# Sparse attention with routed experts on one core: the mask added by TensorE in PSUM, the row shift by VectorE, and the work resequenced

## The chip, the core and the metric

One NeuronCore of a Trainium2 chip. Its engines run in parallel, each through its own instructions in program order: TensorE (PE) multiplies matrices into PSUM, VectorE (DVE) and ScalarE (ACT) work on SBUF and PSUM, GpSimd (POOL) on SBUF, and SyncE (SP) issues most DMAs. The metric is the device time of one execution in microseconds (us).

## The reference

Attention over 8 batches of 8 heads, 576 positions, 64 features. Heads 0 to 3 see the last 32 positions (a local mask), heads 4 to 7 see every 32nd earlier position (a strided mask). Per batch a gate score picks 128 of the 576 rows, which pass a two-layer network and are added back, weighted by a sigmoid.

```python
scores = scale * np.matmul(q, k.transpose(0, 1, 3, 2))
mask_local = (rel >= 0) & (rel < stride)
mask_strided = (rel >= 0) & (pos[None, :] % stride == pos[:, None] % stride)
scores = np.where(masks[None, :, :, :], scores, -1000000000.0)
scores = scores - np.max(scores, axis=-1, keepdims=True)
attn = np.exp(scores)
attn = attn / (np.sum(attn, axis=-1, keepdims=True) + 1e-09)
out = np.matmul(attn, v)
...
for b in range(B):
    top_idx = np.argpartition(-scores[b], capacity)[:capacity]
    xe = x[b, top_idx]
    ye = np.maximum(xe @ w1, 0.0) @ w2
    g = 1.0 / (1.0 + np.exp(-scores[b, top_idx]))
    out[b, top_idx] = x[b, top_idx] + g[:, None] * ye
```

## The kernel before

The 8 batches are taken as 4 groups of two. A group has four pairs of heads (two strided, S, then two local, L), and each pair is cut into two units, so there are 32 units. A unit holds both heads of a pair (h = 0, 1) for 6 or 5 chunks of 128 query rows (S) or 5 or 4 (L). Only the key columns that a mask lets through are computed: 54 columns a chunk for S, 64 for L.

A unit goes through these steps, which have letters in a string `ORDER`:

- `s`, scores: TensorE multiplies small blocks (64 rows of the array, 32 or 64 columns) into two PSUM banks of pool `ps_s`, one for each head (line L241). VectorE adds the mask from PSUM into SBUF tile `sb` (L254) and takes the maximum of each row and chunk, `mx` (L250); GpSimd subtracts it in `sb` (L251).
- `e`: ScalarE takes the exponential (L266; unit 0 does it in two halves, L257).
- `t`: TensorE transposes 4 to 6 blocks through the one bank of `ps_t` (L284), four and then the rest, each copied out by ScalarE to `at` (L285).
- `v`: TensorE multiplies with the values (L313), ScalarE copies out to `xr` (L318, L320).
- `n`: VectorE takes the reciprocals of the sums (L331, L332), GpSimd scales (L334).
- `g`: for the second pair of a kind VectorE forms the gate scores chunk by chunk, instruction `gt` (L348), and SP stores the attention output.

The step `c` advances the ranking of a group: scores brought into order, `rl` transposes (L432), comparisons `b` on VectorE (L470), counting matmuls `bl` on TensorE (L455), one-hot rows (L490), a matmul that picks row numbers, and two gathers by GpSimd's indirect DMA. After it an expert of that group can run: transposes `xt` (L547), 8 hidden chunks `ph` of 12 matmuls (L565), output `po` in 4 parts of 12 matmuls (L581), and a scatter (L588). The letters `f` and `F` advance experts, `w` the split of the weights into two parts (ScalarE L192, GpSimd L194, L198), `q`, `l` and `r` issue the loads of queries and keys, of values and of weights on SP's queue.

`ORDER` sets the program order of all engines at once: each letter emits the next piece of its kind, and where a piece needs another that has not been emitted, that one is emitted first. Buffers limit how far kinds may run ahead of each other: `NSB = 3` score tiles, 2 tiles `at`, `XR = 2`, `QKS = 2` query and key tiles, `RINGS = 4` value tiles.

Of the kernel before, what the change touches and what calls it, by code (L numbers as in the profile page):

```python
# [9 lines left out]
F32 = mybir.dt.float32  # L10
# [37 lines left out]
def attention_then_expert(ctx: ExitStack, tc, capacity, qkL, qkS, vL, vS, w1, w2, consts, consts16, outL, outS):  # L48
# [5 lines left out]
    ps_s = ctx.enter_context(tc.tile_pool(name="ps_s", bufs=2, space=PSUM))  # L54
    ps_t = ctx.enter_context(tc.tile_pool(name="ps_t", bufs=1, space=PSUM))
    ps_a = ctx.enter_context(tc.tile_pool(name="ps_a", bufs=2, space=PSUM))
    ps_c = ctx.enter_context(tc.tile_pool(name="ps_c", bufs=1, space=PSUM))
    ps_f = ctx.enter_context(tc.tile_pool(name="ps_f", bufs=2, space=PSUM))
# [3 lines left out]
    fill = []  # L62
    done = dict.fromkeys("setvngqlrPC", 0)
# [10 lines left out]
    def keep_warm(k):  # L74
        warm = ps_f.tile([P, 512], F32, tag="f", name="warm")
        for _ in range(k):
            ins = pe.matmul(warm, idle, idle[:, None, :].broadcast_to([P, 4, P]), start=True, stop=True)  # L77
# [4 lines left out]
    loaded = {}  # L82

# [48 lines left out]
    maskS = const(QT, "maskS")  # L132
# [6 lines left out]
    done["q"], done["l"] = 2, 3  # L139
# [3 lines left out]
    sizes = 5 * WL, 9 * NCL + 9, NCL * NCS, P * len(rounds), PERMS  # L143
    cuts = [0, *(sum(sizes[: k + 1]) for k in range(5))]
    small = cp.tile([P, cuts[-1]], BF16, name="small")
    nc.sync.dma_start(small, consts16)
    maskL, tab, column, slot, perms = (small[:, x0:x1] for x0, x1 in zip(cuts, cuts[1:]))
    maskL = maskL.rearrange("p (c w) -> p c w", w=WL)
# [19 lines left out]
    split = [0]  # L168

# [3 lines left out]

    def load_weights(i):
        src = halves[i // 2 if i < 4 else i // 4 + 1][0]
        if i < 4:
            n, at = 1024, i % 2 * 1024
            raws[i] = wk.tile([P, n], F32, tag="hl" if i % 2 else "hh", bufs=1, name=f"raw{i}")
        else:
            n, at = 512, i % 4 * 512  # L180
            raws[i] = xes[:, 2 + i % 2]
        nc.sync.dma_start(raws[i], src[:, at : at + n])

    def split_weights():
        for i in range(12):
            complete("r", i)
            _, hi, lo = halves[i // 2 if i < 4 else i // 4 + 1]
            late = None
            for k in range(0, 1024 if i < 4 else 512, 512):
                at = (i % 2 * 1024 if i < 4 else i % 4 * 512) + k  # L190
                cols, raw = slice(at, at + 512), raws[i][:, k : k + 512]
                act.copy(hi[:, cols], raw)  # L192
                if late:
                    pool.tensor_tensor(*late, ALU.subtract)  # L194
                    split[0] += 1
                late = lo[:, cols], raw, hi[:, cols].bitcast(F32)
                yield
            pool.tensor_tensor(*late, ALU.subtract)  # L198
            split[0] += 1
            yield  # L200
# [7 lines left out]
    gated = [0]  # L208
# [3 lines left out]
    def scores(i):  # L212
# [16 lines left out]
        ps = [ps_s.tile([P, 512], F32, tag="s", name=f"s{i}_{h}") for h in range(2)]  # L229
        M = 32 if kind == "L" else 64  # L230
        for c in range(n):
            for x in range(P // M):
# [6 lines left out]
                for h in range(2):  # L239
                    rows = slice(64 * h, 64 * h + 64)  # L240
                    pe.matmul(  # L241
                        ps[h][M * x : M * x + M, c * W : (c + 1) * W],
                        qk[rows, S2 + q0 : S2 + q0 + M],
                        qk[rows, k0 : k0 + W],
                        start=True,
                        stop=True,
                    )

        def shift(part, peak):
            dve.tensor_reduce(peak, part, axis=AX.X, op=ALU.max)  # L250
            pool.tensor_tensor(part, part, peak[..., None].broadcast_to([*peak.shape, W]), ALU.subtract)  # L251

        for h in range(2):
            dve.tensor_tensor(sv[:, h], ps[h][:, : n * W].rearrange("p (c w) -> p c w", w=W), mk, ALU.add)  # L254
            if i == 0:
                shift(sv[:, h], top[:, h])
                act.activation(sv[:, h], sv[:, h], AF.Exp, scale=0.125)  # L257
            yield
        if i:
            shift(sv, top)  # L260
        yield

    def exponentials(i):
        if i:
            sv = live[i][1]
            act.activation(sv, sv, AF.Exp, scale=0.125)  # L266
        yield

    def transposes(i):
# [4 lines left out]
        at = wk.tile([P, 6, P], F32, tag="at", name=f"at{i}")  # L274
# [5 lines left out]
        for k in range(0, len(blocks), 4):  # L280
            part = blocks[k : k + 4]
            pt = ps_t.tile([P, 4, P], F32, tag="t", name=f"t{i}_{k}")
# [3 lines left out]
            yield  # L286

    def values(i):
# [12 lines left out]
        pa = [ps_a.tile([P, 512], F32, tag="a", name=f"a{i}_{k}") for k in range(2)]  # L301
# [14 lines left out]
        for k in range(2):  # L316
# [7 lines left out]
            yield  # L324

    def normalize(i):
# [8 lines left out]
        yield  # L335

    def gates(i):
        g, kind, hp, c0, c1 = units[i]
        if hp == 0:
            return  # L340
# [5 lines left out]
        for c in range(c0, c1):  # L346
            tmp = wk.tile([P, DM // 2], BF16, tag="tmp", bufs=2, name=f"gt{i}_{c}")
            dve.scalar_tensor_tensor(  # L348
                tmp,
                xf[:, c, :],  # L350
                1.0,
                wg[:, w0 : w0 + DM // 2],
                op0=ALU.mult,
                op1=ALU.mult,
                accum_out=gate[g, kind][:, c : c + 1],
            )
            if (c - c0) % 2 and c + 1 < c1:
                yield
# [7 lines left out]
        gated[0] = i + 1  # L366
        yield

    past = {"hidden": 0, "all": 0}
# [13 lines left out]
    def reorder(g):  # L383
        gs = gate[g, "S"]
# [3 lines left out]
        yield  # L388
# [4 lines left out]
        yield  # L393
        pt = ps_c.tile([P, 4, P], F32, tag="c", name=f"rs{g}")[:, 0, : 3 * NCL]
# [4 lines left out]
        yield  # L399
# [22 lines left out]
    def choose(g):  # L422
        score = wk.tile([P, NCL], F32, tag="score", bufs=1, name=f"score{g}")
        dve.tensor_tensor(score, gate[g, "L"][:, :NCL], natural[g], ALU.add)
        yield
        row = wk.tile([P, S2], F32, tag="row", bufs=1, name=f"row{g}")
        for k in range(0, NCL, 4):
            m = min(4, NCL - k)
            pool_, tag = (ps_c, "c") if not k else (ps_s, "s") if g == NG - 1 else (ps_c, "c") if g else (ps_f, "f")
            pt = pool_.tile([P, 4, P], F32, tag=tag, name=f"rl{g}_{k}")  # L430
# [3 lines left out]
            yield  # L434
# [7 lines left out]
        below = ps_c.tile([P, 4, P], F32, tag="c", name=f"bl{g}")[:, 0, :NCL]  # L442
# [20 lines left out]
        for group in rank_groups:  # L463
# [19 lines left out]
            yield  # L483
        earlier(0)
        yield
        dve.tensor_tensor(rank, rank, below, ALU.add)
        for rd, (r0, m) in enumerate(rounds):
            hot = row.bitcast(BF16)[:, :S2].rearrange("p (c k) -> p c k", k=P)
            for c in range(0, NCL, 3):
# [6 lines left out]
                yield  # L496
            idx = wk.tile([P, 2, 2], I32, tag="idx", bufs=4, name=f"idx{g}_{rd}")
            gt = wk.tile([P, 2], F32, tag="gt", bufs=4, name=f"gate{g}_{rd}")
            pt = ps_c.tile([P, 4, P], F32, tag="c", name=f"ip{g}_{rd}")
            picked = pt.rearrange("p a b -> p (a b)")[:m, :18]  # L500
# [12 lines left out]
            yield  # L513
            if g == 1:
                weights_up_to(16)
            while past["all"] < g - 1:
                take(fill)
            for bb in range(2):
                xe = xes[:, 2 * (g % 2) + bb]
# [8 lines left out]
                if bb and rd == len(rounds) - 1:  # L528
                    fill.append(expert(g))
                    done["C"] += 1  # L530
                yield


    def expert(g):
        last = g == NG - 1
        for rd, (r0, m) in enumerate(rounds):
            n = 2 * m
            while past["hidden"] < g:
                take(fill)
# [295 lines left out]
```

## Time and profile before

| | |
|---|---|
| time, median of 3 runs | 284.45 us (283.52 to 285.22) |
| time of the profiled execution | 281.86 us |
| its span, first to last instruction | 280.1 us |
| busy: TensorE, VectorE, GpSimd, ScalarE | 224.7, 186.0, 155.2, 102.2 us |
| mean granted TensorE clock | 0.858 |
| bytes moved by DMA | 54.18 MB |

The profile is of one execution. Busy time is the time in which an engine has an instruction of the program running. The granted clock is the share of the full TensorE clock in a stretch; it is a mean over two levels, full and half.

### The profile page before, as it was taken

What the parts mean: (1) busy time and instruction counts of PE and PEld (TensorE: products, weight loads), DVE (VectorE), ACT (ScalarE), POOL (GpSimd) and SP (SyncE); (2) the same over time, 40 slices, a digit from 0 to 9 for tenths busy, and PEclk for the clock granted to TensorE, in tenths of its full rate; (3) what the DMA queues carried; (4) which work ended last, traced back from release to release, by engine and by line L of the source; (5) the groups of instructions that cost most, each with busy time, mean ns of one, the idle gap of its engine ahead of it and who ended that gap; (6) DMA issues with size and microseconds to landing.
All of it is one profiled execution on the core that took longest, in us unless ns stands there. A gap on an engine that the chain in (4) does not pass through costs nothing.

```text
span 280.1 us, 10759 instructions
## 1 busy us (share of the span) xinstructions
PE 224.7 (80%) x4714; PEld 186.6 (67%) x4714; DVE 186.0 (66%) x499; ACT 102.2 (36%) x226; POOL 155.2 (55%) x185
## 2 busy tenths in 40 slices
PE   7675776585865885799778798678999999999990
PEld 3554555464754663697676686467889797989980
DVE  0444284776599799977997976947997676432320
ACT  1343461452552355446425254344342130212110
POOL 5327347365584694958946869737268450522014
PEclk9687796768677597599999569979999999999996
DMA  6979665884966099860957978924302410211002
GB/s 207 412 289 343 266 241 153 315 314 163 311 228 264 22 332 386 302 248 11 357 193 291 319 296 250 349 73 133 112 4 77 191 54 0 63 50 39 2 0 75
DMA packets 12566, 54.18 MB, mean 193 GB/s; under 512 B 2104, under 2 KB 2232, under 8 KB 9656
## 3 DMA queue, kind: packets, MB, share of 16 engines
q1 hardware_dynamic: 10984, 49.30, 49.0%
q0 software_dynamic: 1536, 4.20, 4.4%
q8 instruction: 37, 0.61, 0.9%
q14 instruction: 9, 0.07, 0.1%
HBM read 41.81 MB, written 11.68 MB: 191 GB/s over the span
## 4 chain that ended last, share of the span: by engine, by line
PE 54%; DVE 21%; issue 15%; ACT 5%; POOL 2%; DMA 1%; POOLq 0%; ACTq 0%; DVEq 0%
PE ph L565 12%; PE po L581 10%; PE s L241 9%; PE a L313 9%; PE t L284 8%; DVE gt L348 6%; DVE b L470 5%; DVE sb L254 3%; DVE mx L250 3%; DVE row L490 2%; ACT at L285 2%; PE warm L77 2%; DVE xes L585 1%; PE rl L432 1%; PE xt L547 1%
## 5 line engine op out<-in xcount | busy, mean ns | idle before, releaser
L251 POOL TENSOR_TENSOR sb<-sb,mx 128x540 f32<-128x540 f32 (+4 forms) x33 | 39.5, 1198 | 33.2 <-DVE mx L250 20.9
L241 PE MATMUL s<-qk 64*32 64x64 f32 (+1 forms) x1856 | 39.2, 262 | 12.9 <-issue 7.8
L284 PE MATMUL t<-ident,sb 128*128 128x128 f32 x168 | 37.7, 343 | 12.1 <-ACT at L285 10.0
L241 PEld LDWEIGHTS s<-qk 64*32 64x32 f32 (+1 forms) x1856 | 31.8, 143 | 20.9 <-issue 11.8
L313 PE MATMUL a<-v,at 64*32 64x65 f32 (+1 forms) x1856 | 36.2, 250 | 9.7 <-issue 9.7
L565 PE MATMUL ph<-xl,w1h 128*128 128x256 f32 x128 | 38.2, 299 | 3.2 <-DVE hl L567 1.7
L285 ACT COPY at<-t 128x512 f32<-128x512 f32 (+2 forms) x56 | 26.9, 480 | 37.2 <-PE t L284 36.8
L313 PEld LDWEIGHTS a<-v,at 64*32 64x32 f32 (+1 forms) x1856 | 30.0, 134 | 15.5 <-issue 13.8
L565 PE MATMUL ph<-xh,w1h 128*128 128x256 f32 x128 | 36.8, 287 | 0.0
L565 PE MATMUL ph<-xh,w1l 128*128 128x256 f32 x128 | 36.8, 287 | 0.0
L284 PEld LDWEIGHTS t<-ident,sb 128*128 128x128 f32 x168 | 22.3, 167 | 20.0 <-ACT at L285 13.7
L334 POOL TENSOR_TENSOR xS<-xr,r 128x768 f32<-128x768 f32 (+1 forms) x16 | 22.0, 1379 | 19.4 <-DVE r L332 18.6
L470 DVE SCALAR_TENSOR_TENSOR b<-row,score,band 128x576 bf16<-128x576 f32 (+9 forms) x40 | 29.8, 778 | 3.5 <-ACT row L433 3.4
L566 ACT ACTIVATE hh<-ph 128x256 fp32r<-128x256 f32 x32 | 12.3, 385 | 45.5 <-PE ph L565 45.4
L334 POOL TENSOR_TENSOR xL<-xr,r 128x640 f32<-128x640 f32 (+1 forms) x16 | 19.0, 1191 | 17.3 <-DVE r L332 10.3
L254 DVE TENSOR_TENSOR sb<-s,maskS 128x324 f32<-128x324 f32 (+1 forms) x32 | 14.1, 455 | 21.1 <-PE s L241 21.0
L348 DVE SCALAR_TENSOR_TENSOR gt<-xS,wg 128x256 bf16<-128x256 f32 x44 | 27.6, 664 | 0.0
L581 PE MATMUL po<-w2h,hh 128*128 128x512 f32 (+1 forms) x68 | 27.5, 405 | 0.0
L565 PEld LDWEIGHTS ph<-xl,w1h 128*128 128x128 f32 x128 | 25.1, 196 | 2.4 <-DVE hl L567 2.0
L565 PEld LDWEIGHTS ph<-xh,w1h 128*128 128x128 f32 x128 | 25.1, 196 | 1.7 <-issue 1.6
L581 PE MATMUL po<-w2h,hl 128*128 128x512 f32 (+1 forms) x68 | 26.1, 384 | 0.0
L567 DVE SCALAR_TENSOR_TENSOR hl<-ph,hh 128x256 fp32r<-128x256 f32 x32 | 13.4, 422 | 19.0 <-ACT hh L566 18.9
(79 smaller groups left out, 409.6 us busy)
## 6 DMA issues: line engine op xcount, KB each, us to landing
qk<-in_qkL SPq DMA_DIRECT2D x8, 1152.0 KB, 8.1
qk<-in_qkS SPq DMA_DIRECT2D x7, 1152.0 KB, 8.3
v<-in_vS SPq DMA_DIRECT2D x16, 390.0 KB, 6.7
v<-in_vL SPq DMA_DIRECT2D x8, 650.0 KB, 7.5
out_s<-xS SPq DMA_DIRECT2D x8, 594.0 KB
out_l<-xL SPq DMA_DIRECT2D x4, 1152.0 KB
v<-in_vL SPq DMA_DIRECT2D x8, 520.0 KB, 6.2
raw<-in_w SPq DMA_DIRECT2D x4, 512.0 KB
```

What stands on the lines that cost most here:

```text
L241: pe.matmul(ps[h][M * x : M * x + M, c * W : (c + 1) * W], qk[rows, S2 + q0 : S2 + q0 + M], qk[rows, k0 : k0 + W], start=True, stop=True,)
L251: pool.tensor_tensor(part, part, peak[..., None].broadcast_to([*peak.shape, W]), ALU.subtract)
L254: dve.tensor_tensor(sv[:, h], ps[h][:, : n * W].rearrange("p (c w) -> p c w", w=W), mk, ALU.add)
L284: pe.transpose(out=pt[:, x, :], in_=block, identity=ident)
L285: act.copy(at[:, k : k + len(part), :], pt[:, : len(part), :])
L313: pe.matmul(pa[k][rows, to * E1 : (to + 1) * E1], at[part, y, rows], v[part, block + step * q], start=True, stop=True)
L334: pool.tensor_tensor(x.rearrange("p c h d -> p h c d"), xr, r, ALU.mult)
L348: dve.scalar_tensor_tensor(tmp, xf[:, c, :], 1.0, wg[:, w0 : w0 + DM // 2], op0=ALU.mult, op1=ALU.mult, accum_out=gate[g, kind][:, c : c + 1],
L470: dve.scalar_tensor_tensor(beats[pp, x1 : x1 + S - s0], row[pp, bb * S + s0 : (bb + 1) * S], score[pp, c : c + 1], band[pp, pp.start - at ...
L565: pe.matmul(ph[:, :n], w[:, f0 // 4, dc, fs], x_[:, dc, :n], start=k == 0, stop=k == len(terms) - 1)
L567: dve.scalar_tensor_tensor(hl[:, fc, :n], ph[:, :n], 0.0, hh[:, fc, :n].bitcast(F32), op0=ALU.max, op1=ALU.subtract)
L581: pe.matmul(po, a[:, fc, cols], w[:, f0 + fc, d0:d1], start=k == 0, stop=k == len(terms) - 1)
```

## The change

The masks are kept in bf16 with an identity matrix in one tile, `lead`, that is loaded in place of the earlier mask tile. For each unit and head a matmul of the identity with the mask opens the accumulation in the score bank, and the score matmuls add to it. VectorE then takes the maximum and the difference from PSUM, head by head; GpSimd no longer takes part in the scores, and unit 0 has no two-part form. The steps become streams that state what they wait for; the expert is three streams (`x` transposes, `h` hidden, `o` output). PSUM banks per pool are the same; the last expert's `xt` and the later `rl` use other pools. The weights come in 16 loads of 512 columns with 3 tiles of their own; before, 4 loads of 1024 and 8 of 512 columns went through tiles of the expert. There are more buffers, and the order is a new string.

```diff
-    sizes = 5 * WL, 9 * NCL + 9, NCL * NCS, P * len(rounds), PERMS
+    first16 = P + QT + 5 * WL
+    lead = cp.tile([P, first16], BF16, name="lead")
+    nc.sync.dma_start(lead, consts16[:, :first16])
+    ident16, maskS, maskL = lead[:, :P], lead[:, P : P + QT], lead[:, P + QT :].rearrange("p (c w) -> p c w", w=WL)
...
-        ps = [ps_s.tile([P, 512], F32, tag="s", name=f"s{i}_{h}") for h in range(2)]
+        ps = [bank("s", f"s{i}_{h}") for h in range(2)]
+        for h in range(2):
+            pe.matmul(ps[h][:, : n * W].rearrange("p (c w) -> p c w", w=W), ident16, mk, start=True, stop=False)
...
-                        start=True,
-                        stop=True,
+                        start=False,
+                        stop=c == n - 1,
                     )
 
-        def shift(part, peak):
+        for h in range(2):
+            part, peak = ps[h][:, : n * W].rearrange("p (c w) -> p c w", w=W), top[:, h]
             dve.tensor_reduce(peak, part, axis=AX.X, op=ALU.max)
-            pool.tensor_tensor(part, part, peak[..., None].broadcast_to([*peak.shape, W]), ALU.subtract)
-
-        for h in range(2):
-            dve.tensor_tensor(sv[:, h], ps[h][:, : n * W].rearrange("p (c w) -> p c w", w=W), mk, ALU.add)
-            if i == 0:
-                shift(sv[:, h], top[:, h])
-                act.activation(sv[:, h], sv[:, h], AF.Exp, scale=0.125)
-            yield
-        if i:
-            shift(sv, top)
-        yield
+            dve.tensor_tensor(sv[:, h], part, peak[..., None].broadcast_to([P, n, W]), ALU.subtract)
+            if not h:
+                yield True
...
+    def load_weights():
+        for i, (src, _, _, cols) in enumerate(pieces):
+            yield [("w", i - RAWS + 1)]
+            raws[i] = wk.tile([P, 512], F32, tag="raw", bufs=RAWS, name=f"raw{i}")
+            nc.sync.dma_start(raws[i], src[:, cols])
+            done["r"] += 1
...
-                pool_, tag = (ps_s, "s") if last else (ps_f, "f")
...
+                pt = bank("x", f"xt{u}_{bb}").rearrange("p (c k) -> p c k", c=4)
...
+        "s": (range(nu), scores, lambda i: [("q", i // 2 + 1), ("t", i - NSB + 1), ("P", int(i == 4))]),
+        "e": (range(nu), exponentials, lambda i: [("s", i + 1)]),
+        "t": (range(nu), transposes, lambda i: [("e", i + 1), ("v", i - ATS + 1)]),
+        "v": (range(nu), values, lambda i: [("t", i + 1), ("l", i + 1), ("n", i - XR + 1), ("g", 0 if i % 4 else i - 4)]),
...
+    def step(kind):
+        for other, k in wants[kind] or ():
+            while done[other] < k:
+                step(MARKS.get(other, other))
+        wants[kind] = next(streams[kind], None)
...
-XR = 2
-QKS = 2
-RINGS = 4
+BANKS = {"s": 2, "t": 1, "a": 2, "c": 1, "f": 2}
+SHARED = {"x": "f", "p": "s"}
+XR = 3
+GATE_DVE = "LS"
+GC = 3
+ATS = 3
+QKS = 3
+RINGS = 5
+RAWS = 3
+HB = 1
...
 ORDER = (
...
+    "ssqrsrlsetPtewsvwssvtstrweseltvseqntssvntvvntestsgrwrgvsqeswtvtgvnlssvvegvtnlstetsvgnvlqnsrlsqetvgrl"
+    "tgwqvntsslvgctleggcsverstctgctvnvssnctvvceenscvseccssccwvttlvqsswvrwtctelvlcntvqstscevctnrvnlsetvllt"
+    "vqtscncersrstqcgsclelstcgggggvvtwrwqesxntcsvvtxvctgevsslglrghnvcslqsghgtcwrhnvleshwvcsongewcoeclntsv"
+    "sctvocgntvstnsvvolleecghgwvcrgtlvccgnsqnhsvvlhttvqcvcccthwotccgsscetcvlcevnggtsseogtvcgcnxtnsvntcxsg"
+    "vcvogcvcoetchcchtvhlnsshoeccovcgtglccncovnovvnchgghghhogccxccocgggcxoochchccchchchocccooccccohchchhocx"
+    "oxoohhhhoooohhhhoooo"
 )
 LAG = 2
-NSB = 3
+NSB = 4
```

## Rows read from the trace of the kernel before

**Rows 1.** The page, busy time of each engine.

```profile
PE 224.7 (80%) x4714; PEld 186.6 (67%) x4714; DVE 186.0 (66%) x499; ACT 102.2 (36%) x226; POOL 155.2 (55%) x185
```

**Rows 2.** Busy time of each engine by stretch, then PEclk, DMA share, GB/s.

```profile
0.00:80.00 80.00, 55.74 (x1625) 41.39 (x1625) 42.91 (x116) 32.96 (x70) 41.12 (x56) 0.79 0.77 278
80.00:160.00 80.00, 62.83 (x1658) 53.16 (x1659) 71.42 (x170) 36.34 (x80) 57.59 (x57) 0.81 0.67 239
160.00:212.00 52.00, 45.22 (x990) 37.61 (x993) 40.37 (x124) 21.23 (x49) 33.51 (x40) 0.90 0.50 174
```

**Rows 3.** The chain in order of time: start us, us, what.

```profile
7.26 0.49 DVE mx L250
...
13.79 1.31 PE a L313 x48
15.11 1.06 PE t L284 x4
...
114.54 2.56 PE ph L565 x12
...
211.57 0.79 PE a L313 x53
...
231.67 2.79 PE po L581 x12
```

**Rows 4.** Waits of TensorE: us in total, times, longest us.

```profile
PE t L284 <- ACT at L285: 10.0, 12, 2.7
PE a L313 <- issue: 9.7, 5, 3.1
PE s L241 <- issue: 7.8, 6, 3.0
PE rl L432 <- DVE score L424: 3.4, 1, 3.4
PE bl L455 <- DVE b L470: 3.1, 3, 2.2
```

**Rows 5.** The page, shares of the chain that ended last.

```profile
PE 54%; DVE 21%; issue 15%; ACT 5%; POOL 2%; DMA 1%; POOLq 0%; ACTq 0%; DVEq 0%
```

**Rows 6.** Two short stretches, columns as in rows 2.

```profile
114.50:117.10 2.60, 2.60 (x21) 2.38 (x26) 2.60 (x5) 0.37 (x1) 2.60 (x3) 0.50 0.78 302
231.70:234.50 2.80, 2.80 (x15) 2.06 (x13) 1.76 (x10) 0.39 (x1) 0.00 (x0) 1.00 0.00 0
```

**Rows 7.** Groups by line: count, busy us, mean ns, idle before, releasers.

```profile
L251 POOL TENSOR_TENSOR sb<-sb,mx 128x540 f32<-128x540 f32 (+4 forms) x33 | 39.5, 1198 | 33.2 <-DVE mx L250 20.9 <-DVE r L331 9.7 <-DVE rank L486 1.6
L470 DVE SCALAR_TENSOR_TENSOR b<-row,score,band 128x576 bf16<-128x576 f32 (+9 forms) x40 | 29.8, 778 | 3.5 <-ACT row L433 3.4
L348 DVE SCALAR_TENSOR_TENSOR gt<-xS,wg 128x256 bf16<-128x256 f32 x44 | 27.6, 664 | 0.0
L348 DVE SCALAR_TENSOR_TENSOR gt<-xL,wg 128x256 bf16<-128x256 f32 x36 | 25.2, 736 | 1.2 <-POOL xL L334 1.2
L250 DVE TENSOR_REDUCE mx<-sb 128x10 f32<-128x540 f32 (+4 forms) x33 | 24.3, 736 | 1.1
L254 DVE TENSOR_TENSOR sb<-s,maskS 128x324 f32<-128x324 f32 (+1 forms) x32 | 14.1, 455 | 21.1 <-PE s L241 21.0
L254 DVE TENSOR_TENSOR sb<-s,small 128x320 f32<-128x320 f32 (+1 forms) x32 | 13.5, 445 | 18.8 <-PE s L241 18.6
```

**Rows 8.** Timeline of VectorE, 101 to 106 us: start, us, instruction.

```profile
101.69 3.43 DVE L348 SCALAR_TENSOR_TENSOR gt<-xS,wg 128x256 bf16<-128x256 f32 x1
...
105.05 0.41 DVE L348 SCALAR_TENSOR_TENSOR gt<-xS,wg 128x256 bf16<-128x256 f32 x1
```

**Rows 9.** Timeline of GpSimd there: first and last of four without a gap.

```profile
100.29 1.05 POOL L334 TENSOR_TENSOR xL<-xr,r 128x512 f32<-128x512 f32 x1
...
103.56 1.27 POOL L251 TENSOR_TENSOR sb<-sb,mx 128x648 f32<-128x648 f32 x1
```

**Rows 10.** Groups by line: the one-column matmuls of the ranking.

```profile
L455 PE MATMUL bl<-minus,b 128*128 128x1 bf16 (+2 forms) x80 | 6.9, 174 | 3.4 <-DVE b L470 3.1
```

More of the change, by code (lines that the diff above doesn't have):

```diff
@@ L53, in attention_then_expert, with bank @@
     wk = ctx.enter_context(tc.tile_pool(name="wk", bufs=2))
[L54 to L58, printed above, removed]
+    pools = {
+        tag: ctx.enter_context(tc.tile_pool(name="ps_" + tag, bufs=bufs, space=PSUM)) for tag, bufs in BANKS.items()
+    }
+    def bank(tag, name):
+        tag = SHARED.get(tag, tag)
+        return pools[tag].tile([P, 512], F32, tag=tag, name=name)
     E = mybir.EngineType
     ctx.enter_context(tc.manual_schedule(engines=MANUAL(E)))
-    fill = []
-    done = dict.fromkeys("setvngqlrPC", 0)
     rounds = [(r0, min(P, capacity - r0)) for r0 in range(0, capacity, P)]
@@ L300, in values @@
         M = 32 if kind == "L" else 64
-        pa = [ps_a.tile([P, 512], F32, tag="a", name=f"a{i}_{k}") for k in range(2)]
+        pa = [bank("a", f"a{i}_{k}") for k in range(2)]
         if kind == "L":
@@ L512, in choose @@
             dve.reciprocal(gt[:m], gt[:m])
[L513 to L517, printed above, removed]
             for bb in range(2):
+                yield [("o", 2 * len(rounds) * (g - 1))]
                 xe = xes[:, 2 * (g % 2) + bb]
@@ L527, in choose, with expert_tokens @@
                 chosen[g, rd, bb] = idx, gt, xe
[L528 to L539, printed above, removed]
-            xh = wk.tile([P, 4, 2 * P], F32R, tag="xh", bufs=1, name=f"xh{g}_{rd}")
-            xl = wk.tile([P, 4, 2 * P], F32R, tag="xl", bufs=1, name=f"xl{g}_{rd}")
-            for bb in range(2):
+            done["C"] += 1
+    turns = [(g, rd, r0, m) for g in range(NG) for rd, (r0, m) in enumerate(rounds)]
+    inner = {}
+    def expert_tokens():
+        for u, (g, rd, r0, m) in enumerate(turns):
+            want = [("C", u + 1), ("h", u)]
+            for bb in range(2):
+                yield want
+                if not bb:
+                    xh = wk.tile([P, 4, 2 * P], F32R, tag="xh", bufs=1, name=f"xh{u}")
+                    xl = wk.tile([P, 4, 2 * P], F32R, tag="xl", bufs=1, name=f"xl{u}")
+                want = []
                 xe = chosen[g, rd, bb][2]
-                pool_, tag = (ps_s, "s") if last else (ps_f, "f")
-                pt = pool_.tile([P, 512], F32, tag=tag, name=f"xt{g}_{rd}_{bb}").rearrange("p (c k) -> p c k", c=4)
+                pt = bank("x", f"xt{u}_{bb}").rearrange("p (c k) -> p c k", c=4)
                 for dc in range(4):
@@ L593, in expert, with stream, once, run @@
                                 )
-                    if f0 and bb and rd == len(rounds) - 1:
-                        past["all"] += 1
-                    yield
-    def take(queue, k=1):
-        while k > 0 and queue:
-            try:
-                next(queue[0])
-                k -= 1
-            except StopIteration:
-                queue.pop(0)
-    def weights_up_to(k):
-        while split[0] < k:
-            take(weights)
+                done["o"] += 1
+    def stream(kind, items, make, needs):
+        for i in items:
+            want, pieces_, more = needs(i), make(i), True
+            while more:
+                yield want
+                more, want = next(pieces_, False), []
+            done[kind] = i + 1
+    def once(f):
+        def run(i):
+            f(i)
+            yield from ()
+        return run
     def prepare(_):
```

287 lines of the change are left out of this document (122 added, 165 removed).

## The prediction

> **What bounds the kernel now.** I read the page's first part, then the granted clock and busy time by stretch, the waits of TensorE, the chain that ended last, the groups of instructions by line, and last single instructions in the timeline.
>
> TensorE is the busiest engine: 224.7 of 280.1 us, the VectorE 186.0, GpSimd 155.2 [rows 1]. The stretches show that no engine is full before 212 us [rows 2]: TensorE works 70 to 87% of each of the three stretches at a granted clock of 0.79 to 0.90, a mixture of the levels 1.2 and 2.4 GHz. VectorE is light in the first stretch (42.9 of 80 us) and nearly full in the second (71.4 of 80). By 212 us the last value matmuls of L313 have run [rows 3], and what follows is expert work of the last groups.
>
> So the time is TensorE's work plus its waits plus a tail. The waits [rows 4]: 17.5 us of "issue" (nothing in the profile releases it), 10.0 us of transposes for ScalarE's copy out of the single `ps_t` bank, 6.5 us for VectorE in the ranking (`rl`, `bl`). A wait of TensorE for GpSimd's subtraction is not among the large ones. The chain that ended last agrees: TensorE 54%, VectorE 21%, GpSimd only 2% [rows 5].
>
> The work behind the last value matmul (20 hidden chunks and 10 output parts by the new order string, one chunk fewer in the old) stays nearly the same, so the change is decided ahead of it.
>
> **The change, part by part.** The sum is made against the profiled execution, 281.86 us of its own (span 280.1, 1.8 around it). That run lies 2.6 us under the median of 284.45; I apply the difference to the median.
>
> *Mask matmuls.* 64 matmuls are added, two per unit, with a mean of 292.5 columns ((324+270+320+256)/4) of one pass. Twelve `po` matmuls of 512 columns took 2.79 us, 0.454 ns a column, and twelve `ph` of 256 took 2.56, 0.833 ns [rows 3]; the granted clock was 1.00 in the one stretch and 0.50 in the other [rows 6]. That is 0.133 or 0.244 us a mask. The clock averages 0.825 over the three stretches [rows 2], so 35% of the time is at the lower level: 0.172 us, times 64 = +11.0 us (8.5 to 15.6). Their weight loads run beside other matmuls and are put at nothing; one that lay open would be part of the shape rival below. Some of the 17.5 us of issue waits may run out while a mask is multiplied: -2 (0 to -5).
>
> *VectorE.* Out go the additions, 14.1 + 13.5 us, and the reductions from SBUF, 24.3 us [rows 7]. In come 64 subtractions out of PSUM with one operand in SBUF, as the additions were, so 27.6 us again; and 64 reductions out of PSUM over one half unit. The nearest row is a reduction of 324 columns from SBUF, that of unit 0, 0.49 us [rows 3]; scaled to 292.5 columns it is between 0.44 (all of it by columns) and 0.49, I take 0.465 and 29.8 us. Reading PSUM should not add: the additions read it and average 0.45 us over the same widths [rows 7]. Net +5.5 us of VectorE.
>
> *What GpSimd no longer blocks.* One `gt` instruction took 3.43 us, the next of the same shape 0.41 [rows 8]; the long one ended as a run of four GpSimd operations without a gap ended, two of them the subtraction of L251 (first and last shown) [rows 9]. The 80 `gt` average 0.664 and 0.736 us [rows 7], so 44 x 0.254 + 36 x 0.326 = 22.9 of 55.7 us are such blocking, 41%. The same share of the 40 `b` (31.1 us) is 12.8. L251 is 39.5 of GpSimd's 155.2 us, a quarter, and half of the one run seen: 9 to 18 us of 35.7, I take 13. The additions, whose one operand is in PSUM, average 0.45 us over 256 to 324 columns [rows 7], less than one `gt` of 256 with its blocking; the new subtraction has its operands where they had them, so I count no blocking of it. VectorE's net is +5.5 - 13 = -7.5 us. It is on the chain for 21%, 59 of 186 us, so at least a third (-2.5), at most all counts; as VectorE is nearly full in the second stretch I take -5.
>
> *The hop through GpSimd.* It has 2% of the chain, 5.6 us, of which I give L251 about half: -3 (0 to -5.6). The rest of its 39.5 us was hidden by other units' work on TensorE.
>
> *Transposes.* The waits for the copy came 12 times, 10.0 us. In the new order string 9 units have their two transpose groups next to each other on TensorE, the others have values, scores or expert work between: 9 x 0.83 = 7.5, so -2.5 (0 to -4). The single bank remains.
>
> *A new wait.* A unit's scores fill both `ps_s` banks. VectorE let go of them after two additions (2 x 0.45 us); now after reduction, subtraction, reduction, subtraction, 2 x (0.49 + 0.45) = 1.9 us [rows 3, 7]. The mask matmul of the next unit waits for that on TensorE, and everything behind it in order (transposes, values, expert matmuls) waits along. In the new order most of the first 17 units have one or one and a half transpose groups and one unit's values between two units' scores; one value stage took 1.31 us and one transpose group 1.06 in the cold first stretch [rows 3], and at the upper level less, so 1.2 to 2.4 us. A shortfall of up to 0.7 us in 16 places would be 11 us; part falls where TensorE waits for issue anyway. I take +4 (0 to +11).
>
> *Ranking.* `rl` behind `score` and `bl` behind `b` wait 6.5 us [rows 4]. In the new order there is a whole unit's scores or values, over 1 us, between the last rank group and `earlier(0)`, and between `score` and the first `rl`: -5 (0 to -6.5).
>
> *Clock.* 35% of 212 us at the lower level with TensorE 77% busy is 57 us of work; by the two column prices it would save up to 57 x (1 - 0.454/0.833) = 26 us at the upper one. Masks and fewer waits make TensorE denser; I take a seventh, -4 (0 to -26).
>
> *Start.* The first matmul now needs `lead` (502 two-byte columns, 128 KB) where VectorE needed a mask of 27 KB: 101 KB at 278 GB/s [rows 2] is +0.4. The exponentials of unit 0 lose their two-part form, and two VectorE operations replace GpSimd's: nothing net.
>
> *Priced at nothing.* Deeper buffers (`NSB`, `ATS`, `XR`, `QKS`, `RINGS`) and 16 weight loads instead of 12 on SP's queue: TensorE's waits for a load are too short to stand among [rows 4], because the loads are issued a unit or more ahead. SP's queue is in order: loads also stand behind the stores of `gates`, which wait for GpSimd's normalisation. If that lead goes, each late load is a stall of microseconds on TensorE. The last group's `xt` and `rl` in other banks: enough expert matmuls lie ready beside them.
>
> Sum: 11.0 - 2 - 5 - 3 - 2.5 + 4 - 5 - 4 + 0.4 = -6.1 us. Span 274.0, own time 275.8, on the median 278.3: 278.
>
> **Rivals.**
>
> *The clock follows (faster).* If TensorE gets dense enough to hold the upper level for two thirds of the work that now runs at the lower one, the clock term is -17: 265 us. For it: the second stretch, where VectorE is relieved, runs at 0.81. Against: the first stretch has the same low clock and its waits are mostly issue, which the change does not touch.
>
> *Hidden anyway (no change).* GpSimd is on 2% of the chain; if half of the freed VectorE time is slack (-2.5) and the new order keeps half of the ranking's waits (-2.5) and a clock term of -3, the sum is -0.1: 284 us. For it: TensorE, not GpSimd, is what the attention units queue for. Against: the second stretch, where VectorE has no slack.
>
> *The score banks (slower).* If the shortfall of 0.7 us is met at three quarters of the 31 successions, the wait is 16.5 us in place of 4: 291 us. It decides from 10 us on (0.33 us a unit), where it eats the gain. For it: the new string leaves less between two units' scores than 212 / 32 = 6.6 us, the old pace of a unit; against: the old waits of scores for VectorE are too small to be in [rows 4], and later units have expert work between.
>
> *The change of shape (slower).* Each unit's scores use 64-row pieces of the array, the mask all of it; twice a unit TensorE may run empty. A one-column matmul takes 174 ns [rows 10], so 64 changes expose at most 11.1 us: 289 us. It decides from 6 us, 0.1 us a change. The Trainium skill (TensorEngine Tiling (Array Packing), "Key Properties") states that changing the tiling mode drains TensorE, which speaks for this rival; no run here shows the price of a drain yet.
>
> **How the numbers follow.** Chances: forecast 0.44 (own range 268 to 282.5), clock 0.15, hidden 0.13, banks 0.17, shape 0.11. Half a per cent, 1.4 us, is about what a measurement of this kernel tells from no change: faster 0.59, same 0.13, slower 0.28. The range goes from the clock rival to the bank rival, 263 to 291; outside remain a half of the clock's and a part of the banks' chance.
>
> **What would show it.** Masks: 64 matmuls of 0.13 to 0.25 us. VectorE: `gt` averages near 0.55 instead of 0.70, busy time near 178. Banks: TensorE's wait of the mask for VectorE, 4 us in all if I am right, over 10 if not. Transposes waiting for the copy: 7.5 us. Ranking waits under 2 us. Clock: 0.81 to 0.84 in the first two stretches; over 0.9 would be the first rival. The forecast would be wrong if loads appear among TensorE's waits, or if issue waits grow.

## The result, and the profile after

The changed kernel took 272.81 us (median of 4 runs, 270.63 to 275.63), the kernel before 283.99 (4 runs, 283.14 to 285.22) beside it: a ratio of 0.9714, with a 95% interval of 0.9646 to 0.9783. Run again later it took 272.56 (6 runs) against 281.91 (17 runs): 0.9694 (0.9636 to 0.9752). The profiled execution took 272.86 us of its own, span 271.0: 9.0 less than the profiled one before, where the sum had said 6.1 less. Ratios leave out every execution that took over 1.5% more than the fastest of its kernel.

The first part of the page of the changed kernel, busy times by engine:

```profile
PE 229.9 (85%) x4778; PEld 185.7 (69%) x4778; DVE 166.5 (61%) x530; ACT 101.4 (37%) x225; POOL 115.9 (43%) x154
```

Against [rows 1] the 64 masks are TensorE's only new matmuls (4714 to 4778). VectorE is 19.5 us lighter, GpSimd 39.3.

Stretches of the changed kernel (length; busy time and number for TensorE, its weight loads, VectorE, ScalarE, GpSimd; then clock, DMA share, GB/s), and under them the value matmuls L295, with their first and last start:

```profile
0.00:80.00 80.00, 59.39 (x1630) 42.63 (x1630) 41.94 (x128) 32.79 (x68) 29.91 (x46) 0.74 0.84 312
80.00:160.00 80.00, 68.13 (x1824) 54.84 (x1822) 58.15 (x197) 39.20 (x87) 37.20 (x41) 0.87 0.66 235
160.00:200.00 40.00, 39.23 (x892) 32.49 (x888) 34.52 (x112) 17.20 (x40) 22.95 (x32) 1.00 0.45 165
200.00:271.00 71.00, 63.12 (x443) 55.76 (x439) 31.89 (x95) 12.21 (x31) 25.83 (x37) 0.98 0.16 55
```

```profile
L295 PE MATMUL a<-v,at x1856: 213/219/368, 14.8 to 199.5; 64*32 64x65 f32 x116, 64*64 64x65 f32 x70
```

The same row of the kernel before:

```profile
L313 PE MATMUL a<-v,at x1856: 213/219/367, 13.6 to 212.1; 64*32 64x65 f32 x116, 64*64 64x65 f32 x70
```

The last value matmul starts at 199.5 us, before at 212.1. That is 12.6 us gained ahead of the tail; the tail from there is 71.5 us long and was 68.0, which gives 3.5 back. TensorE stood idle 20.6 + 11.9 + 0.8 = 33.3 us up to 200 us. Before, with the stretches of [rows 2], it was 24.3 + 17.2 + 6.8, some 48 us, up to 212. So 15 us of idle time are gone, 11 of them after 80 us, and TensorE's busy time ahead of the tail grew only from 163.8 to 166.8 us although it multiplies the masks. The granted clock fell in the first stretch (0.79 to 0.74) and rose in the second (0.81 to 0.87) and third (0.90 to 1.00).

TensorE's waits in the changed kernel (waiting line, releaser, us in total, times, longest):

```profile
PE a L295 <- issue: 16.2, 10, 3.2
PE t L265 <- ACT at L266: 7.5, 13, 1.5
PE s L218 <- DVE sb L241: 4.0, 5, 1.3
PE s L230 <- issue: 1.6, 2, 1.1
PE s L218 <- DVE score L415: 1.2, 1, 1.2
...
PE bl L433 <- ACT row L423: 0.5, 1, 0.5
PE s L218 <- DMA lead<-in_consts: 0.3, 1, 0.3
```

Against [rows 4]: the ranking's 6.5 us are down to 1.7 (1.2 of it now in front of a mask), the transposes' 10.0 are 7.5, the masks wait 4.0 for VectorE to free the score banks, and issue stands at 17.8 where it was 17.5 in the two large rows.

What these issue waits are can be read from the single transfers in the packed trace. Queue q8 brings instructions, by its size TensorE's: 37 transfers for its 9556 matmuls and weight loads, and 38 in e5 below, which has 128 more. The row of the changed kernel (transfers, MB, share of the DMA engines' time):

```profile
q8 instruction: 37, 0.61, 0.9%
```

In all 14 traces together TensorE's matmuls have 122 issue waits of over 0.8 us (9 here). All but two end 1.2 to 1.6 us after a transfer of q8 has ended, while of 145 equally long waits with another cause 11 do. So the issue waits are TensorE waiting for its own next instructions, and the change leaves them as long as they were.

Groups of instructions of the changed kernel (busy us, mean ns of one, idle time before and its releaser):

```profile
L240 DVE TENSOR_REDUCE mx<-s 128x6 f32<-128x324 f32 (+3 forms) x64 | 29.0, 453 | 41.7 <-PE s L230 41.7
L241 DVE TENSOR_TENSOR sb<-s,mx 128x324 f32<-128x324 f32 (+3 forms) x64 | 29.6, 463 | 2.6
L330 DVE SCALAR_TENSOR_TENSOR gt<-xS,wg 128x256 bf16<-128x256 f32 x44 | 20.8, 518 | 1.6 <-POOL xS L317 1.6
L330 DVE SCALAR_TENSOR_TENSOR gt<-xL,wg 128x256 bf16<-128x256 f32 x36 | 15.0, 461 | 0.0
L460 DVE SCALAR_TENSOR_TENSOR b<-row,score,band 128x576 bf16<-128x576 f32 (+9 forms) x40 | 22.3, 598 | 0.1
L218 PE MATMUL s<-lead 128*128 128x324 bf16 (+3 forms) x64 | 17.8, 352 | 5.6 <-DVE sb L241 4.0 <-DVE score L415 1.2 <-DMA lead<-in_consts 0.3
```

The `gt` fell from 664 and 736 ns to 518 and 461, `b` from 778 to 598 [rows 7]. The chain that ended last:

```profile
PE 56%; issue 16%; DVE 9%; DMA 9%; ACT 4%; POOL 3%; SPq 1%; POOLq 0%; ACTq 0%
```

VectorE's 21% [rows 5] are now 9%; GpSimd was small on the chain and still is. DMA had 1% and now has 9%, 24 us: two loads in the first 20 us, and after 200 us a gather and two scatters of the experts. The loads, start and us:

```profile
4.32 7.74 DMA v<-in_vS
12.08 7.73 DMA raw<-in_w
```

TensorE does not wait for them directly. ScalarE does, 4.8 us in front of the first weight split, and its copies for the attention units stand behind that split.

### The profile page after: what moved, and what is told of

It is laid out like the page before. It is cut to its first block, busy times and chain, and to the rows that moved or that the text cites. A ratio compares the mean times of both kernels' runs of the same rounds, so it can differ in the third digit from the quotient of the medians.

```text
span 271.0 us, 10834 instructions
## 1 busy us (share of the span) xinstructions
PE 229.9 (85%) x4778; PEld 185.7 (69%) x4778; DVE 166.5 (61%) x530; ACT 101.4 (37%) x225; POOL 115.9 (43%) x154
## 4 chain that ended last, share of the span: by engine, by line
PE 56%; issue 16%; DVE 9%; DMA 9%; ACT 4%; POOL 3%; SPq 1%; POOLq 0%; ACTq 0%
PE po L578 10%; PE ph L554 10%; PE a L295 10%; PE s L230 9%; PE t L265 8%; PE s L218 3%; DVE gt L330 3%; DMA v<-in_vS 3%; DMA raw<-in_w 3%; ACT at L266 2%; PE rl L422 2%; DMA out_l<-xes,idx 2%; DVE sb L241 2%; PE bl L445 2%; DMA xes<-out_s,idx 2%
## 5 line engine op out<-in xcount | busy, mean ns | idle before, releaser
L240 DVE TENSOR_REDUCE mx<-s 128x6 f32<-128x324 f32 (+3 forms) x64 | 29.0, 453 | 41.7 <-PE s L230 41.7
L295 PE MATMUL a<-v,at 64*32 64x65 f32 (+1 forms) x1856 | 37.6, 251 | 16.3 <-issue 16.2
L295 PEld LDWEIGHTS a<-v,at 64*32 64x32 f32 (+1 forms) x1856 | 30.5, 134 | 23.9 <-issue 22.6
L265 PE MATMUL t<-ident,sb 128*128 128x128 f32 x168 | 36.2, 333 | 8.6 <-ACT at L266 7.5
L230 PEld LDWEIGHTS s<-qk 64*32 64x32 f32 (+1 forms) x1856 | 29.5, 137 | 14.1 <-issue 13.0
L230 PE MATMUL s<-qk 64*32 64x64 f32 (+1 forms) x1856 | 35.3, 250 | 1.7 <-issue 1.6
L265 PEld LDWEIGHTS t<-ident,sb 128*128 128x128 f32 x168 | 21.9, 163 | 14.9 <-ACT at L266 10.3
L241 DVE TENSOR_TENSOR sb<-s,mx 128x324 f32<-128x324 f32 (+3 forms) x64 | 29.6, 463 | 2.6
L578 PE MATMUL po<-w2h,hl 128*128 128x512 f32 (+1 forms) x68 | 25.9, 381 | 0.0
L578 PE MATMUL po<-w2l,hh 128*128 128x512 f32 (+1 forms) x68 | 25.9, 381 | 0.0
L556 DVE SCALAR_TENSOR_TENSOR hl<-ph,hh 128x256 fp32r<-128x256 f32 x32 | 13.4, 420 | 19.5 <-ACT hh L555 19.2
L554 PEld LDWEIGHTS ph<-xl,w1h 128*128 128x128 f32 x128 | 24.1, 188 | 0.6
L554 PEld LDWEIGHTS ph<-xh,w1h 128*128 128x128 f32 x128 | 24.2, 189 | 0.2
L554 PEld LDWEIGHTS ph<-xh,w1l 128*128 128x128 f32 x128 | 24.1, 188 | 0.0
```

Source lines behind the costliest of these rows:

```text
L230: pe.matmul(ps[h][M * x : M * x + M, c * W : (c + 1) * W], qk[rows, S2 + q0 : S2 + q0 + M], qk[rows, k0 : k0 + W], start=False, stop=c == ...
L241: dve.tensor_tensor(sv[:, h], part, peak[..., None].broadcast_to([P, n, W]), ALU.subtract)
L265: pe.transpose(out=pt[:, x, :], in_=block, identity=ident)
L295: pe.matmul(pa[k][rows, to * E1 : (to + 1) * E1], at[part, y, rows], v[part, block + step * q], start=True, stop=True)
L554: pe.matmul(ph[:, :n], w[:, half, dc, fs], x_[:, dc, :n], start=k == 0, stop=k == len(terms) - 1)
L556: dve.scalar_tensor_tensor(hl[:, fc, :n], ph[:, :n], 0.0, hh[:, fc, :n].bitcast(F32), op0=ALU.max, op1=ALU.subtract)
```

## The experiments

The theory was that of the prediction's sum: the mask move costs TensorE more than it gives VectorE and GpSimd (+5.4 us together), and the new order and buffers earn more than that back (-11.5). The rival: the mask move earns most of it, and the order little. Three groups of runs on three chips; the kernel before ran beside each.

### The two halves of the change alone

`e1_old_mask_new_order` is the changed kernel with the old mask step:

```diff
-            pe.matmul(ps[h][:, : n * W]..., ident16, mk, start=True, stop=False)
...
-            dve.tensor_reduce(peak, part, axis=AX.X, op=ALU.max)
-            dve.tensor_tensor(sv[:, h], part, peak[..., None].broadcast_to([P, n, W]), ALU.subtract)
+            dve.tensor_tensor(sv[:, h], part, mk, ALU.add)
...
+        dve.tensor_reduce(top, sv, axis=AX.X, op=ALU.max)
+        pool.tensor_tensor(sv, sv, top[..., None].broadcast_to([*top.shape, W]), ALU.subtract)
```

> The changed kernel with the mask step of before (VectorE adds the mask out of PSUM and takes the maximum in SBUF, GpSimd subtracts), in the new order with the new buffers. By my own sum the move of the mask alone costs (+11 masks, -2 issue, -5 VectorE, -3 hop, +4 banks, +0.4 start = +5.4 us) and the order gains, so this runs at 265 to 270 us, below the changed kernel's 272.8. The rival, that the move of the mask is what pays and the order only carries it, expects 278 to 284 us: `gt` back near 0.65 us, VectorE busy near 185.

`e2_new_mask_old_order` is the kernel before with only the mask move: `lead`, the mask matmul ahead of the scores, and maximum and subtraction from PSUM by VectorE, in the old order with the old buffers.

> The kernel before with the mask added by TensorE and the maximum and difference taken from PSUM, in the old order with the old buffers and steps. By my sum 284 + 5.4 = 289 us (285 to 292). The rival, that the move pays by itself, expects 274 to 280 us. In both VectorE's busy time falls to about 165 to 175 us.

Measured: e1 281.42 us, ratio to the kernel before 0.9965 (0.9907 to 1.0023); e2 282.62, ratio 0.9907 (0.9816 to 0.9999). The order with its buffers gives nothing alone that this measurement can tell, the mask move alone about 1% at the edge of what it can tell, and the two together 3%. The theory's ranges, 265 to 270 and 285 to 292 us, were both missed, so its split is wrong. The rival's range held for e1 (278 to 284) and not for e2 (274 to 280). A plain sum of two terms would be 0.987 (0.976 to 0.998 from the two intervals) and misses the measured 0.969 to 0.971, if not by much. Waits of ScalarE and of TensorE in e1, and under them its value matmuls:

```profile
ACT sb L245 <- POOL sb L241: 25.9, 11, 7.5
```

```profile
PE t L263 <- ACT at L264: 12.2, 13, 2.4
...
PE rs L385 <- POOL spread L379: 3.8, 2, 2.0
PE ph L552 <- issue: 2.8, 1, 2.8
PE s L228 <- DVE mx L240: 2.0, 1, 2.0
```

```profile
L293 PE MATMUL a<-v,at x1856: 213/267/368, 14.1 to 209.9; 64*32 64x65 f32 x116, 64*64 64x65 f32 x70
```

In e1 the exponentials wait 25.9 us for GpSimd's subtraction (13.1 in the kernel before, in two rows), the transposes wait 12.2 us, and TensorE waits 3.8 us for `spread`, a GpSimd step of the ranking. The waits that the order was to remove (`rl`, `bl`) are no longer among the large ones, but others have come, and the last value matmul starts at 209.9 us, nearly as late as before.

### GpSimd's work given back, with nothing waiting for its result

`e4_gpsimd_work_back` and `e4b_gpsimd_work_back` (the same kernel on another chip): the changed kernel, and after each unit GpSimd subtracts the maxima in a spare tile that nobody reads.

```diff
+        scr = spare[:, : 2 * n * W].rearrange("p (h c w) -> p h c w", h=2, w=W)
+        pool.tensor_tensor(scr, scr, top[..., None].broadcast_to([P, 2, n, W]), ALU.subtract)
```

> The changed kernel, and for each unit GpSimd also does a subtraction of the size of the removed one on a spare tile that nobody reads. It tests blocking alone: GpSimd is busy for 40 us more, VectorE's own work is the same. If the freed blocking counted as I put it, VectorE's busy time rises by 9 to 18 us (`gt` from 0.49 to about 0.65) and the time to 276 to 280 us. The rival, that this VectorE time is slack, expects the same rise of VectorE and 272 to 274 us.

> The changed kernel with a subtraction of the old size by GpSimd for each unit on a spare tile, once more with more runs, because its first times lay between 274.8 and 281.4 us. If what GpSimd took from VectorE is most of the gain: 278 to 282 us. If the 274.8 is the rule and the others the exception: 274 to 276 us.

`e8_gpsimd_memsets`: GpSimd reads one column of the maxima, so that it waits at the same place, and then only writes for as long.

```diff
+        pool.tensor_copy(probe, top[:, 1, n - 1 : n])
+        for _ in range(2):
+            pool.memset(spare, 0.0)
```

> As the run before, but the work that GpSimd does for each unit only writes: it copies one column of the maxima, so that it waits for VectorE as the subtraction did, and then fills a spare tile twice (about as long in all). GpSimd's queue is as full as with the subtraction, but it does not read through SBUF while it works. If VectorE being blocked by GpSimd's reads is the cause, `gt` stays near 0.49 us and the time at 271 to 275 us. The rival, that GpSimd's own queue delays the normalisation and the weights, expects the time of the subtraction run, 278 to 282 us, with `gt` near 0.49 us all the same.

Measured: e4 281.14 us (4 runs: three at 281.0 to 281.4, one at 274.8; before there 283.0), e4b 283.43 and e8 283.24 (6 runs each), 0.943 and 0.948 of the kernel before on their chip. All three lie just above the ranges expected for a loss.

How large the loss is, is less sure than that e4b and e8 are equal. The changed kernel was not run beside e4, nor beside e4b and e8. On the chip of e4b and e8 the kernel before took 299.7 us, 6% more than elsewhere; if that chip slowed the changed kernel as much, it would take some 289 us there and the added work would cost nothing. Against that stands that this same kernel took about as long on the other chip (e4, three of four), where the kernel before took its usual 283.0. Set against 272.6 to 272.8 elsewhere, the work then costs some 8.5 us (e4) to 11 (e4b, e8), although nothing uses its result. The one run of e4 at 274.8 us stays unexplained; by it alone the loss would be 2 us. The six of e4b lie at 280.4 to 286.5.

Undoing the mask move costs about the same in e1 (281.42 - 272.56 = 8.9, on two chips), though e1 also loses the masks' effect on the clock, so the two losses need not be the same loss. A hop through GpSimd on the units' own path is not needed for the loss in e4. One tie is left: GpSimd now reads the maxima, of which there are three tiles, and VectorE can overwrite a tile only afterwards. Waits of VectorE's maximum for GpSimd are absent in e4 and e4b; e8 has one, 2.3 us.

Groups of e4b, then the same of e8:

```profile
L247 POOL TENSOR_TENSOR spare<-spare,mx 128x648 f32<-128x648 f32 (+3 forms) x32 | 37.9, 1185 | 25.9 <-DVE mx L242 22.9 <-DMA raw<-in_w 2.4 <-DMA out_l<-xL 0.4
...
L334 DVE SCALAR_TENSOR_TENSOR gt<-xS,wg 128x256 bf16<-128x256 f32 x44 | 27.1, 661 | 2.4 <-POOL xS L321 2.4
```

```profile
L249 POOL MEMSET spare<- 128x500 f32 x64 | 32.9, 514 | 1.8
...
L336 DVE SCALAR_TENSOR_TENSOR gt<-xS,wg 128x256 bf16<-128x256 f32 x44 | 21.4, 533 | 2.4 <-POOL xS L323 2.3
```

With the subtraction `gt` takes 661 ns, as in [rows 7]; with memsets 533, nearly the 518 of the changed kernel. VectorE's busy time is 187.0 and 171.5 us. Yet both kernels take the same time, on the same chip. So 15.5 us of blocked VectorE time were worth nothing here. What is left as the cause, by exclusion, is that GpSimd's queue is occupied, and made to wait for the maxima, in front of its other work; occupation and waiting were not tested apart. The last value matmul starts at 209.0 and 207.8 us. Which of the queued steps is the one that matters was not isolated. TensorE's wait for `spread` is there in e1 (3.8 us), e4 (2.0), e4b (1.5) and e8 (2.2) and absent from the changed kernel's list, but it is too short for 9 us. The chains differ too; of e8 and of e4b:

```profile
PE 51%; issue 18%; DVE 9%; DMA 8%; POOL 7%; ACT 3%; SPq 1%; POOLq 0%; ACTq 0%; DVEq 0%
```

```profile
PE 57%; issue 17%; DVE 10%; DMA 7%; ACT 3%; POOL 3%; SPq 1%; POOLq 0%; ACTq 0%; DVEq 0%
```

GpSimd's share of the chain is 7% of 280.6 us, 20 us, in e8, 8% in e4 and 9% in e1, against 3%, 8 us, in the changed kernel. But it is 3% in e4b, and 6% in e6 below, which has none of the added work, so the chain of one execution does not settle the path.

### What a mask costs

`c_changed_again` is the changed kernel on this group's chip. `e5_mask_twice` adds a second matmul of the same shape behind each mask, of a tile of zeros; `e6_no_mask` leaves the masks out, and nothing takes their place.

> The changed kernel once more, unaltered, as the measure for the three others on the same chip: 270 to 275 us.

```diff
             pe.matmul(ps[h][:, : n * W]..., ident16, mk, start=True, stop=False)
+            pe.matmul(ps[h][:, : n * W]..., idle, mk, start=False, stop=False)
```

> The changed kernel with a second matmul behind each mask matmul, of the same shape and columns, that adds zeros. It adds the column price once more and no change of shape. If TensorE's work is on the path, by the column price (0.133 to 0.244 us, 64 times) 8 to 13 us: 280 to 285 us. If the masks run where TensorE would wait for issue anyway, 273 to 276 us.

```diff
-            pe.matmul(ps[h][:, : n * W]..., ident16, mk, start=True, stop=False)
...
-                        start=False,
-                        stop=c == n - 1,
+                        start=True,
+                        stop=True,
```

> The changed kernel without the mask matmuls; the mask is left out of the computation and nothing takes its place. It takes away the columns and the two changes of shape of each unit. By the column price alone 11 us less: about 262 us. With a shape price of up to 0.17 us a change up to 22 us less: 251 to 262 us. If the masks were hidden: 269 to 273 us.

`e7_mask_in_score_shape` gives the strided units' masks in the shape of their scores, 64-row pieces of the array; the local units stay as they are.

```diff
+                    rows = slice(64 * h, 64 * h + 64)
+                    pe.matmul(part[64 * x : 64 * x + 64], ident16[rows, rows], mk[rows], start=True, stop=False)
```

> The changed kernel, with the masks of the 16 strided units multiplied in the pieces of the array that the scores use (64 rows by 64 columns, two pieces for each head in place of one matmul of the whole array). The change of shape goes for half of the units and the pieces of the two heads can run side by side; 32 matmuls more are issued. If the change of shape costs something: 3 to 6 us less than the changed kernel, 267 to 270 us. If it costs nothing: 272 to 275 us.

Measured: the changed kernel again 272.56 us; masks twice 282.28, ratio to before 1.0006 (0.9958 to 1.0054), so 9.7 us more by the medians (8.8 by the ratios), or 0.14 to 0.15 us for each of 64; no masks 273.3 (4 runs, 267.8 to 277.9), ratio 0.9587 (0.9481 to 0.9693). The second mask costs its full column price, as expected (8 to 13 us). The first is nearly free: by the ratios taking it away gains 1.1% (3 us; the intervals allow from nothing to 6), and by the medians nothing, where 11 us or more would have been the price of the columns.

The pages show where the first mask's time comes back. Busy times of the changed kernel on this chip, and of e6:

```profile
PE 227.4 (84%) x4778; PEld 183.7 (68%) x4778; DVE 168.8 (63%) x530; ACT 101.5 (38%) x225; POOL 116.9 (43%) x154
PE 224.0 (82%) x4714; PEld 186.0 (68%) x4714; DVE 162.8 (60%) x530; ACT 101.3 (37%) x225; POOL 116.1 (43%) x154
```

With the masks TensorE is busy only 3.4 us longer, although they alone take 15.0 us from start to start: its other matmuls take 11.6 us less. It stands idle 42.0 us with them (span 269.4) and 49.0 without (273.0). TensorE's largest waits without masks, and those of the changed kernel on the same chip:

```profile
PE a L293 <- issue: 13.0, 8, 4.9
PE s L228 <- issue: 10.8, 5, 4.1
```

```profile
PE a L295 <- issue: 18.9, 11, 3.9
PE t L265 <- ACT at L266: 7.3, 13, 1.3
PE s L218 <- DVE sb L241: 4.8, 6, 1.4
```

Issue is 23.8 us without masks and 19.2 with them (18.9 here and 0.3 in front of L230), and the granted clock of the profiled execution 0.858 without and 0.895 with. So the masks are paid back mostly by the higher granted clock of all other matmuls, and in part by shorter waits. This is one execution of each, and that of e6 (274.9 us) is not among its fastest. But the clocks of all runs agree: 0.893 to 0.917 in six with masks, 0.858 to 0.867 in four without. The masks do not hold the clock up whatever the waits are: in e3, e9 and e10 below, with masks and fewer buffers, it is 0.80 to 0.85. The second mask found nothing more to gain: 0.900 in the profiled execution of e5.

e7 took 275.34 us (6 runs, 268.27 to 277.57), a scatter too wide for a verdict; it shows no gain from keeping the shape. The traces show why there is little to gain. Starts on TensorE around one unit's masks in the changed kernel, at granted clock 1.00, and under them the same place in e6 (start, us, what):

```profile
173.78 0.27 PE L265 MATMUL t<-ident,sb 128*128 128x128 f32 x1
173.89 0.30 PE L218 MATMUL s<-lead 128*128 128x320 bf16 x1
174.03 0.30 PE L218 MATMUL s<-lead 128*128 128x320 bf16 x1
174.26 0.30 PE L230 MATMUL s<-qk 64*32 64x64 f32 x10
```

```profile
175.96 0.27 PE L263 MATMUL t<-ident,sb 128*128 128x128 f32 x1
176.16 0.27 PE L228 MATMUL s<-qk 64*32 64x64 f32 x6
```

From a mask to a mask it takes 0.14 us, from a mask to a score tile 0.23: 0.09 us more. Without masks the step from the whole-array transpose to the score tile takes 0.20, where transpose to mask takes 0.11: again 0.09 more. So the change from the whole array to 64 rows has a price, but 25 of the 31 later units pay it in e6 too, because a whole-array matmul stands in front of their scores.

### The buffers

`e3_old_buffers` puts the old depths into the changed kernel; `e9_nsb3` changes `NSB` alone, `e10_old_buffers_but_nsb` all but that:

```diff
-XR = 3
+XR = 2
...
-ATS = 3
-QKS = 3
-RINGS = 5
+ATS = 2
+QKS = 2
+RINGS = 4
...
-NSB = 4
+NSB = 3
```

> The changed kernel with the buffer counts of before (NSB 3, ATS 2, XR 2, QKS 2, RINGS 4); a step whose buffer is not free pulls the step that frees it forward, so the order shifts by that. I priced the buffers at nothing: 272 to 275 us. The rival, that the buffers carry the gain, expects 278 to 284 us and loads or copies among TensorE's waits.

> The changed kernel with 3 score tiles instead of 4, all other buffers as changed. If the score tiles are what the new order cannot do without, most of the 52 us that the old buffer counts cost are here: 300 to 325 us. If it is the loads' buffers or the others: 272 to 280 us.

> The changed kernel with 4 score tiles and the other buffers as before (ATS 2, XR 2, QKS 2, RINGS 4). The counterpart of the run with 3 score tiles: if the score tiles carry it, 273 to 285 us; if the others do, 300 to 325 us.

Measured: e3 325.18 us, ratio 1.1472 (1.1394 to 1.155), 52 us over the changed kernel, which was not run beside it. On the chip where the kernel before took 299.7, e9 took 330.71 (1.1073, 1.0969 to 1.1176) and e10 329.74 (2 runs each); that is 46 us or more over e4b on the same chip. All three lie beyond every range expected. Either half is enough to lose all. TensorE's waits in e3:

```profile
PE t L265 <- ACT at L266: 10.4, 13, 2.2
PE s L218 <- DVE sb L241: 9.8, 12, 1.6
PE bl L445 <- DVE b L460: 8.5, 8, 2.0
PE t L265 <- ACT sb L247: 5.5, 7, 1.3
PE a L295 <- issue: 4.4, 6, 1.2
PE a L295 <- DMA v<-in_vL: 4.1, 1, 4.1
```

Every kind of wait is back, one for a load among them. A step whose buffer is missing makes `step` emit the steps that free it first, so another program order comes out of the same string. Whether that order costs the time, or the missing buffers themselves, was not tested apart.

## Why the prediction was right, and where its working was not

The sign, the range and, within 6 us, the time were right (278 predicted, 272.8 measured; between the profiled executions 6.1 us less predicted, 9.0 measured). The working was right for some terms and wrong for others that cancelled, so that the sum came out as near as it did is in part luck.

- **Masks.** Predicted +11.0 on TensorE with 2 hidden. Read in the timeline from start to start, waits taken out, a mask takes about 0.20 us at the upper clock level and 0.31 at the lower, 15.5 us for 64, the top of the bounds. A mask in front of another takes the predicted column price (medians 0.14 and 0.24 us); the one in front of a score tile takes 0.22 and 0.38. In time it is 0 to 3 us (e6). The step that failed is that TensorE's added work was put on the path nearly whole, -2 for waits and -4 for the clock against it; by the pages of e6 and the changed kernel 11.6 us of other work and 7 us of idle time came back. The second mask (e5) costs close to what had been taken for the first: 0.15 against 0.172 us.
- **VectorE and its blocking.** Busy time 166.5 where 178 was predicted, `gt` near 0.49 us where 0.55 was: `gt` and `b` together are 23.5 us shorter (16.3 and 7.2), where 13 was taken from bounds of 9 to 18. Its value of -5 was mis-placed: e8 against e4b shows no time for 15.5 us of it, with GpSimd's queue as full in both.
- **GpSimd.** Predicted -3, from its 2% of the chain [rows 5]; the runs put it at -8.5 to -11 (e4, e4b, e8), measured across chips as said above. With that reservation this is the other term that was mis-sized, and "The rest of its 39.5 us was hidden" did not hold in the new order. In the old order all of the mask move gives only about 1% (e2).
- **Transposes, ranking, score banks.** Their waits came out at 7.5 us (7.5 predicted), 1.7 (under 2) and 4.0 (4). As rows they were right. As times they were not: e1 has the new order without the ranking's old waits and is no faster; by its rows the waits moved to GpSimd and ScalarE.
- **Clock.** 0.74 and 0.87 in the first two stretches where 0.81 to 0.84 was predicted (0.78 and 0.87 in the run again); over the span 0.858 became 0.880, and 0.895 in the run again. The term of -4 was too small: in the changed kernel all matmuls but the masks take 229.9 - 15.5 = 214.4 us, 10.3 less than before. The profiled executions of the new order without masks ran at 0.823 (e1) and 0.858 (e6), those with them at 0.891, 0.900 and 0.894 even with GpSimd's work given back (e4, e4b, e8). So the masks go with the higher level, and the order alone does not: TensorE is busy 231.4 us in e1 and 229.9 in the changed kernel, which has 64 matmuls more.
- **Start.** The first mask starts at 5.5 us and waits 0.3 us for `lead`; 0.4 was predicted. The first value matmul starts 1.2 us later than before (14.8 against 13.6), which had no term.
- **Buffers at nothing.** As far as TensorE's waits for loads go this held: none stands among the large ones, though two loads stand on the chain at the start. As an edit it did not: without them the new order costs 52 us (e3).
- **Rivals.** The score banks' 10 us were not met (4.0, and 4.8 in the run again), nor the 11.1 us of the change of shape: e6 leaves some 3 us, at most 6, for masks and changes together. Where that rival went wrong is that it charged both changes to the masks; most units changed from the whole array to 64 rows already. The Trainium skill (TensorEngine Tiling (Array Packing), "Key Properties") states that a change of mode drains TensorE; the 0.09 us that the traces show for a change to 64 rows agree with that, though the load of the score tile's weights was not tested apart from it. "Hidden anyway" was right that freed VectorE time is slack, and wrong that GpSimd's work was. The clock rose by less than its rival needed.
- **Issue.** The prediction took these waits as released by nothing. They are TensorE's waits for its own instructions, and the masks, 128 more instructions with their weight loads, did not lengthen them (17.5 to 17.8 us).

## What to carry to other kernels

An engine that is on 2% of the chain can still cost some 8 to 11 us through its queue: give its work back with nothing using its result before calling it hidden, beside the unaltered kernel on the same chip (which is missing here), and write as long with memsets to part its queue from the blocking of its neighbour. A TensorE that stood idle for 48 us ahead of the tail took the first 64 matmuls for almost nothing, mostly because its other matmuls then ran at a higher granted clock (one profile of each), and paid in full for the next 64. A price for a change of shape belongs to an added matmul only if the change was not there before. A hand-written order, its buffer depths and its operations are one setting: the parts gave 0 and 1% alone, 3% together, and a single missing score tile lost some 50 us.

## What was not expected of the hardware

The kernel before took 283.0 us (7 runs) and 281.9 (17 runs) on two chips and 299.7 (11 runs) on a third, where two variants of the changed kernel took 283; nothing run here says why.

Two-input VectorE instructions were held back by GpSimd's subtraction and not by its memsets: `gt` 661 against 533 ns at nearly equal GpSimd time (155.8 and 154.0 us). The Trainium skill (SBUF — State Buffer, "Who interferes with whom") states that a VectorE instruction with two inputs in SBUF contends with a GpSimd instruction that reads SBUF and not with one that only writes; the two traces agree.
